# Output stage of the two-slot tiles regrouped: sums of h, state sums, R4 and R5; four sums of the sixth tile on GpSimd

## The chip, the cores and the metric

One NeuronCore of a Trainium2 chip runs the whole kernel in one launch. The metric is device time in microseconds, the median of several runs. Engines are named as in the profile: PE is TensorE (matrix products), DVE is VectorE, ACT is ScalarE, POOL is GpSimd, SP issues the DMAs.

## The reference

A retention recurrence over 4 batches, 8 heads, 768 positions and head size 64, followed by a bilinear feed-forward layer over all 3072 tokens:

```
for t in range(S):
    state = gamma * state + k[:, :, t] outer v[:, :, t]      # per head, 64 x 64
    y[:, :, t] = scale * q[:, :, t] @ state
...
x = y as (3072, 512)
out = ((x @ w_a) * (x @ w_b)) @ w_out                        # d_ff = 1536
```

Inputs and output are float32; the kernel computes products in bfloat16 and adds in float32.

## The kernel before

**Slots and tiles.** The 3072 tokens are 24 slots of 128. `TILES = [4, 2, 2, 2, 2, 4, 4, 4]` groups them into eight tiles, J = 0 to 7; "two-slot tiles" are J = 1 to 4, and the sixth tile is J = 5. J = 2, 3 and 4 follow the same code with a few exceptions for 4. Retention is computed in chunks, two slots at a time, and its result is stored transposed as `xt[J]`, the input of the feed-forward layer of tile J.

**The loop over a tile.** `blocks(J)` goes through twelve steps `ft` (128 columns of d_ff each). In each, `ffn_ab` does `ffn_a` (four products into a PSUM bank "a", cast by ACT to `asb`) and `ffn_g` (four products into a bank "g", which DVE multiplies with `asb` into `ht[J][:, ft]`). Steps in `SPARE` use the attention banks y0 and y1, the others the three rotating banks of the pool `psff`. Then comes the output stage. For tiles in `FAST` it is `ffn_fast(J, u)`, once for each pair of slots u.

**The output stage with seven products.** `ffn_fast` multiplies 2 x 2 blocks with seven products rather than eight (Strassen's scheme in Winograd's form). Each product is six matmuls of 128 x 256. Three use slices of `ht` itself ("h"), four use sums of them ("s", tile `hsum`, four kinds `which` = 0 to 3, each over six column groups f). `add(J, which, f0, f1, eng)` makes the sums for f0 to f1; `adds_of(J, ft)` lists which follow step `ft` (12 is ahead of the output stage, 13 in it, after the first `plus`). The products add into PSUM banks R1, R2, R4 and R5. ACT copies intermediate values of R1 and others to `snap` (`keep`), DVE adds `snap` to a bank into the output tile `osb` (`plus`). R4 exists only for pairs in `ASIDE`; elsewhere its product is the last one, into R1, and ACT copies the result to `osb`. The order with R4 is R1 h00, R2 h10, R4 h11, R1 + s1, R5 s0, R1 + s2, R5 + s3.

**Retention beside it.** `turn(new, old)` does for slots `new` the products of states (`chunk_states`) and scores, and for slots `old` the output products (`inter`, `intra`), which land in the banks y0 and y1. `chunk_states` writes the products to one `psff` bank and to the bank st, and DVE then adds them up into running state sums (`sums`). ACT casts each sum to `gst`, but not at once: the casts wait in a list `later`, and `catch_up(n)` issues the next n of it at given places of the feed-forward code; the two casts of y0 and y1 into `xt` go ahead of them in the list. In the same way the masks of scores wait in `unmasked` for `mask_now`. `casts(t)` scales k and q of slot t and casts v on GpSimd, and issues one transposing DMA on SP; after an odd slot it also issues the loads of the next two.

**What sets the order.** Every instruction goes through `seq`, which chains it to the previous one on its engine: each engine runs in the order in which the program emits. Calls outside the feed-forward loop hang in a table `ahead`, by tile and step, and `visit` runs them there. The tile framework inserts the semaphore waits for data and for buffers that must become free. Tiles 6 and 7 also use seven products for a part of `a` (`SEVEN`, `blocks_seven`), and there some sums of h already run on GpSimd (`sums_of`).

Of the kernel before, what the change touches and what calls it, by code (L numbers as in the profile page):

```python
# [9 lines left out]
F32 = mybir.dt.float32  # L10
BF16 = mybir.dt.bfloat16
AF = mybir.ActivationFunctionType
ALU = mybir.AluOpType
# [1 line left out]

TILES = [4, 2, 2, 2, 2, 4, 4, 4]
FAST = (2, 3, 4, 5, 6, 7)
ASIDE = ((2, 0), (3, 0), (4, 0), (5, 0), (6, 0), (6, 1), (7, 0))
SEVEN = {6: (1, 4), 7: (1, 6)}
SPARE = {(J, ft) for J in (2, 3, 4) for ft in range(1, 6 if J == 4 else 10, 2)}  # L20
PAIRS = 3
# [6 lines left out]
def kernel(  # L28
# [10 lines left out]
    nc = tc.nc  # L39
    P = 128  # L40
    B, H, S, D = q.shape
    NCH = S // P
    HP = H // 2
    DM = H * D
    DFF = moe_w_a.shape[1]
    KT = DM // P
    NFT = DFF // P
# [15 lines left out]
    tra = ctx.enter_context(tc.tile_pool(name="tra", bufs=4))  # L63
# [4 lines left out]
    psat = ctx.enter_context(tc.tile_pool(name="psat", bufs=1, space=bass.MemoryType.PSUM))  # L68
# [6 lines left out]
    def seq(bi):  # L75
        ins = bi.ins
        prev = last.get(ins.engine)
        if prev is not None:
            tc.add_manual_dep(ins, prev.name, nosync, reason="program order")
        last[ins.engine] = ins  # L80
        return bi
# [99 lines left out]
    gst = [const.tile([P, HP, D], BF16, name=f"gst{i}") for i in range(8)]  # L181
# [18 lines left out]
    def cast(engine, dst, src):  # L200
        if engine is nc.scalar:
            seq(nc.scalar.copy(dst, src))  # L202
        else:
            seq(engine.tensor_copy(dst, src))  # L204
# [63 lines left out]
    later = []  # L268
# [6 lines left out]
    sums = {}  # L275

    def chunk_states(n):

        u = [psff.tile([P, 2, HP, D], F32, tag="ff", name="st"),
             psst.tile([P, 2, HP, D], F32, tag="st", name="st")]  # L280
        for s in range(2):
            for hp in range(HP):
                for c in range(2):
                    if (n + s + 1) % NCH == 0 and c == 1:
                        continue
                    for r in range(2):
                        seq(nc.tensor.matmul(u[c][half(r), s, hp, :], kb[n + s][half(c), hp, r, :],  # L287
                                             vb[n + s][half(c), HP * r + hp, :],
                                             start=True, stop=True, skip_group_check=True))
        for s in range(2):  # L290
            t = n + s
            sums[t] = tra.tile([P, 2, HP, D], F32, tag="qk"[s] + "T2", name="sums", bufs=2)
            for c in range(2):
                if (t + 1) % NCH == 0 and c == 1:
                    continue
                new = sums[t][:, c]
                old = sums[t][:, 0] if c else sums.get(t - 1, sums[t])[:, 1]
                if t % NCH == 0 and c == 0:
                    seq(nc.vector.tensor_copy(new, u[c][:, s]))  # L299
                else:  # L300
                    seq(nc.vector.tensor_tensor(new, u[c][:, s], old, op=ALU.add))  # L301
                later.append(lambda i=2 * t + c + 1, new=new: cast(nc.scalar, gst[i % 8], new))

    unmasked = []

# [354 lines left out]
    def add(J, which, f0, f1, eng=nc.vector):  # L660
        if J not in hsum:
            hsum[J] = [wstage.tile([P, NH, 2, P], BF16, tag="w" + "ab"[i % 2], name="hsum") for i in range(4)]
        s = [x[:, f0:f1, : TILES[J] // 2] for x in hsum[J]]
        x, y, op = {
            0: (lambda: rows(J, 0, 1, f0, f1), lambda: rows(J, 1, 1, f0, f1), ALU.add),
            1: (lambda: s[0], lambda: rows(J, 0, 0, f0, f1), ALU.subtract),
            2: (lambda: rows(J, 0, 0, f0, f1), lambda: rows(J, 0, 1, f0, f1), ALU.subtract),
            3: (lambda: rows(J, 1, 0, f0, f1), lambda: s[1], ALU.subtract),
        }[which]
        seq(eng.tensor_tensor(s[which], x(), y(), op=op))  # L670
# [44 lines left out]
    def seven_a(J, f):  # L715

        W2 = 2 * P
        if J not in banks:
            own_banks(J)
        R1, R2, R5 = banks[J][f % 2]  # L720
        snap = raw.tile([P, 4, W2], F32, tag="vf", name="snap")
# [8 lines left out]
        part_a(J, f, R2, 2, True)  # L730
        part_a(J, f, R5, 5, True)
        seq(nc.scalar.copy(snap[:, 2], R5))
        for fn in behind[:1]:
# [41 lines left out]
    def ffn_fast(J, u):  # L775
        osb, dst = placed[J, u] = place(J, u)
        ends = J == len(TILES) - 1 and u == TILES[J] // 2 - 1
        snap = wstage.tile([P, 4, DH], F32, tag="w" + "ba"[u % 2], name="snap")

        def bank():  # L780
            return psff.tile([P, DM], F32, tag="ff", name="o")

        def keep(i, R):
            seq(nc.scalar.copy(snap[:, i], R[:, :DH]))  # L784

        def plus(dst, R, x):
            seq(nc.vector.tensor_tensor(dst, R[:, :DH], x, op=ALU.add))  # L787

        R1, R2 = bank(), bank()
        swap = (J, u) == (7, 0)  # L790
        if swap:
            product(R2, J, u, ("h", 1, 0), (0, 2), True)
        product(R1, J, u, ("h", 0, 0), (0, 0), True)
        keep(0, R1)
        catch_up(2)
        if not swap:
            product(R2, J, u, ("h", 1, 0), (0, 2), True)
        visit(J, "mid")
        plus(osb[:, 0, :DH], R2, snap[:, 0])
        for which, f0, f1 in adds_of(J, NFT + 1):  # L800
            add(J, which, f0, f1)
        mask_now(1)
        catch_up(1)
        store()
        aside = (J, u) in ASIDE
        if aside:
            R4 = bank()
            product(R4, J, u, ("h", 1, 1), (1, 3), True)
            keep(2, R4)
        product(R1, J, u, ("s", 1), (1, 1), False)  # L810
        keep(1, R1)
        catch_up(1)
        visit(J, "sums", u)
        R5 = bank()
        product(R5, J, u, ("s", 0), (1, 0), True)
        keep(3, R5)
        catch_up(1)
        product(R1, J, u, ("s", 2), (1, 2), False)
        if aside:
            seq(nc.vector.tensor_tensor(osb[:, 1].rearrange("p (c d) -> p c d", c=2),  # L820
                                        R1[:, :DH].rearrange("p (c d) -> p c d", c=1).to_broadcast([P, 2, DH]),
                                        snap[:, 2:], op=ALU.add))
        else:
            plus(osb[:, 1, DH:], R1, snap[:, 3])
        if ends:
            seq(nc.sync.dma_start(out=dst[:, 1, DH:], in_=osb[:, 1, DH:]))
        mask_now(1)
        product(R5, J, u, ("s", 3), (0, 3), False)
        plus(osb[:, 0, DH:], R5, snap[:, 1])
        mask_now()  # L830
        if ends:
            seq(nc.sync.dma_start(out=dst[:, 0], in_=osb[:, 0]))
        catch_up(1)
        if not aside:
            product(R1, J, u, ("h", 1, 1), (1, 3), False)
            seq(nc.scalar.copy(osb[:, 1, :DH], R1[:, :DH]))
        if J < len(TILES) - 2:
            held.append((dst, osb))
        elif ends:
            seq(nc.scalar.dma_start(out=dst[:, 1, :DH], in_=osb[:, 1, :DH]))  # L840
        else:
            seq(nc.sync.dma_start(out=dst, in_=osb))

    D_, G_, A_ = nc.vector, nc.gpsimd, nc.scalar
# [100 lines left out]
    for j in range(NO):  # L945
# [8 lines left out]
        (4, 0): [(casts, 17)], (4, 8): [(turn, 14, 12)],  # L954
        (4, "o", 0): [(begin_turn, 14), (casts, 18)], (4, "mid"): [(end_turn, 14), (casts, 19)],
        (5, 0): [(casts, 20)], (5, 2): [(casts, 21)], (5, 3): [(turn, 16, None)],
        (5, 8): [(turn, 18, 16), (casts, 22)],
        (5, "sums", 0): [(turn, 20, 18), (casts, 23)],
        (6, 8): [(turn, 22, 20)], (6, "o", 0): [(turn, None, 22)],
    }  # L960
    ahead[5, "sums", 0] += [(combine_a, f) for f in (1, 2, 3)]
    early = {3: [(0, 0, 2)], 4: [(1, 0, 2)], 5: [(2, 0, 2)], 6: [(3, 0, 2)],
             7: [(0, 2, 4)], 8: [(1, 2, 4)], 9: [(2, 2, 4)], 10: [(3, 2, 4)]}
    adds = {4: {**early, 10: [(3, 2, 4), (0, 4, 5)],
                11: [(1, 4, 5), (0, 5, 6), (1, 5, 6), (2, 4, 5), (2, 5, 6), (3, 4, 5), (3, 5, 6)]},
            2: {**early, 12: [(0, 4, 6), (1, 4, 6)], 13: [(2, 4, 6), (3, 4, 6)]}}

    def visit(*at):
        for fn, *what in ahead.pop(at, ()):
# [2 lines left out]
    def adds_of(J, ft):  # L972
        if J == 4:
            return {4: [(0, 0, 2), (1, 0, 2)], 5: [(2, 0, 2)], 6: [(3, 0, 2)], 10: [(0, 2, 4), (1, 2, 4)],
                    11: [(2, 2, 4), (3, 2, 4)], 12: [(i, 4, 6) for i in range(4)]}.get(ft, ())
        return adds[TILES[J]].get(ft, ())

    def blocks_seven(J):
# [32 lines left out]
    def blocks(J):  # L1011
        done = blocks_seven(J) if J in SEVEN else 0
        for ft in range(done, NFT):
            if ft > 1 or J == 5:
                store()
            visit(J, ft)
            ffn_ab(J, ft)
            if J in FAST:
                for which, f0, f1 in adds_of(J, ft):
                    if J not in SEVEN or f0 >= 4:  # L1020
                        add(J, which, f0, f1)

    combined = {(0, 0): (0, 3), (0, 1): (3, 6)}
    blocks(1)
# [46 lines left out]
```

## Time and profile before

| | |
|---|---|
| median of 3 runs | 221.41 us (221.08 to 221.74) |
| the profiled execution | 221.99 us, of which the span of instructions is 220.3 us |
| PE busy | 212.1 us, 96% of the span |
| DVE busy | 147.8 us, 67% |
| ACT busy | 96.6 us, 44% |
| POOL busy | 116.2 us, 53% |
| granted PE clock | 1.000 |

A row of the timeline has the start in us, the duration, engine, line of the kernel, operation, tiles written and read, form and count (xN: N instructions merged, the duration then goes from the first start to the last end); brackets give the idle time before it and what ended it. A row of a group has the count, the total busy time and the mean duration in ns.

### The profile page before, as it was taken

Reading aid. Unit: us, or ns where it says so; the run is one execution under the profiler, and the core shown is the slowest. Engines: PE = TensorE matmul, PEld = TensorE weight load, DVE = VectorE, ACT = ScalarE, POOL = GpSimd, SP = SyncE. Lnnn points to the kernel's source line nnn. Section 1 sums busy time; section 2 is a strip of 40 time slices with the busy share of each in tenths; the row PEclk is TensorE's granted clock in tenths of the full one; section 3 lists DMA queues with packets and bytes.
Section 4 is the critical chain, followed back from the end, with each engine's and each line's share of the span. In section 5 each row is a group of like instructions: output and inputs, shape, how many; then the busy total and the mean of one; then the engine's idle time right before and its main releaser. Section 6 shows DMA issues by size and latency. Waiting matters only on the chain.

```text
span 220.3 us, 7032 instructions
## 1 busy us (share of the span) xinstructions
PE 212.1 (96%) x2875; PEld 156.5 (71%) x2875; DVE 147.8 (67%) x324; ACT 96.6 (44%) x240; POOL 116.2 (53%) x157
## 2 busy tenths in 40 slices
PE   8889999999999999999999999999999999999993
PEld 7568898886456888887878445478666478666682
DVE  2774456657806687698685489897877694777731
ACT  3665334442426436426466343636432643443231
POOL 6457798682734545054352514536959960087500
PEclk9999999999999999999999999999999999999999
DMA  6999999997999997997868899898800002200022
GB/s 172 346 377 382 369 299 390 342 207 167 216 259 246 233 220 141 128 236 203 191 130 201 230 150 257 156 221 120 237 0 4 0 3 98 97 0 1 3 95 95
DMA packets 94832, 39.77 MB, mean 181 GB/s; under 512 B 76112, under 2 KB 91728, under 8 KB 94800
## 3 DMA queue, kind: packets, MB, share of 16 engines
q1 hardware_dynamic: 94656, 39.20, 70.2%
q8 instruction: 22, 0.36, 0.7%
q10 hardware_dynamic: 144, 0.13, 0.2%
q14 instruction: 10, 0.08, 0.1%
HBM read 28.31 MB, written 6.29 MB: 157 GB/s over the span
## 4 chain that ended last, share of the span: by engine, by line
PE 86%; DVE 5%; DMA 3%; issue 2%; POOL 1%; ACT 1%; SPq 0%; DVEq 0%; POOLq 0%; ACTq 0%
PE g L610 27%; PE a L598 22%; PE o L772 18%; PE o L647 7%; PE a L712 5%; DMA kf<-in_k_dram 3%; DVE ht L613 2%; DVE hsum L670 1%; PE st L287 1%; POOL kqb L239 1%; PE y L359 1%; PE y L371 1%; PE at L317 1%; PE tp L450 1%; PE st L491 1%
## 5 line engine op out<-in xcount | busy, mean ns | idle before, releaser
L613 DVE TENSOR_TENSOR ht<-g,asb 128x256 bf16<-128x256 f32 (+1 forms) x98 | 53.7, 548 | 39.1 <-PE g L610 29.3
L610 PE MATMUL g<-xt,wb_bf 128*128 128x256 bf16 (+1 forms) x432 | 77.7, 308 | 0.3 <-ACT asb L602 0.3
L598 PE MATMUL a<-xt,wa_bf 128*128 128x256 bf16 (+1 forms) x368 | 60.8, 296 | 0.1
L602 ACT CAST asb<-a 128x256 bf16<-128x256 f32 (+1 forms) x82 | 36.8, 450 | 51.4 <-PE a L598 50.8
L610 PEld LDWEIGHTS <-wb_bf 128*128 128x128 bf16 x432 | 42.1, 98 | 16.5 <-issue 0.4
L598 PEld LDWEIGHTS <-wa_bf 128*128 128x128 bf16 x368 | 35.4, 98 | 12.1
L239 POOL TENSOR_TENSOR kqb<-kf,ktab 128x512 bf16<-128x512 f32 x21 | 22.7, 1081 | 40.5 <-DMA kf<-in_k_dram 29.8
L239 POOL TENSOR_TENSOR kqb<-qf,qtab 128x512 bf16<-128x512 f32 x21 | 22.5, 1076 | 6.4 <-DMA qf<-in_q_dram 6.4
L204 POOL CAST vb<-vf 128x512 bf16<-128x512 f32 x24 | 14.8, 624 | 17.8 <-DMA vf<-in_v_dram 13.0
L772 PEld LDWEIGHTS <-hsum 128*128 128x128 bf16 x216 | 21.0, 98 | 4.1 <-DVE hsum L670 0.9
L784 ACT COPY snap<-o 128x256 f32<-128x256 f32 x34 | 12.7, 374 | 21.3 <-PE o L772 19.5
L772 PE MATMUL o<-wt_bf,hsum 128*128 128x256 bf16 x162 | 19.8, 272 | 0.9 <-DVE osb L787 0.5
L670 POOL TENSOR_TENSOR hsum<-ht 128x256 bf16<-128x256 bf16 (+1 forms) x15 | 11.0, 733 | 17.9 <-DVE ht L613 17.9
L772 PEld LDWEIGHTS <-ht 128*128 128x128 bf16 x162 | 15.4, 98 | 2.6
L647 PE MATMUL o<-wo_bf,ht 128*128 128x512 bf16 x72 | 16.1, 379 | 0.0
L670 DVE TENSOR_TENSOR hsum<-ht 128x256 bf16<-128x256 bf16 (+1 forms) x32 | 14.2, 450 | 0.3
L301 DVE TENSOR_TENSOR sums<-st,sums 128x256 f32<-128x256 f32 x30 | 12.7, 423 | 1.5
L772 PE MATMUL o<-wo_bf,ht 128*128 128x256 bf16 x108 | 13.3, 273 | 0.0
L202 ACT CAST gst<-sums 128x256 bf16<-128x256 f32 x33 | 12.6, 412 | 0.5 <-DVE sums L299 0.3
L647 PEld LDWEIGHTS <-ht 128*128 128x128 bf16 x72 | 6.9, 98 | 7.9
L323 DVE TENSOR_TENSOR aT<-at,mask 128x512 bf16<-128x512 f32 x18 | 12.1, 680 | 0.0
L787 DVE TENSOR_TENSOR osb<-o,snap 128x256 f32<-128x256 f32 x20 | 8.3, 416 | 4.8 <-PE o L772 3.2
(99 smaller groups left out, 260.4 us busy)
## 6 DMA issues: line engine op xcount, KB each, us to landing
out_dram<-osb SPq DMA_DIRECT2D x11, 512.0 KB, 3.2
kf<-in_k_dram SPq DMA_DIRECT2D x18, 256.0 KB, 3.9
qf<-in_q_dram SPq DMA_DIRECT2D x36, 128.0 KB, 3.8
vf<-in_v_dram SPq DMA_DIRECT2D x18, 256.0 KB, 4.2
wsta<-in_moe_w_a_dram SPq DMA_DIRECT2D x6, 512.0 KB, 7.6
wstb<-in_moe_w_b_dram SPq DMA_DIRECT2D x6, 512.0 KB, 7.8
wsto<-in_moe_w_out_dram SPq DMA_DIRECT2D x6, 512.0 KB, 8.7
kf<-in_k_dram SPq DMA_DIRECT2D x3, 512.0 KB, 6.1
```

Source lines behind the costliest of these rows:

```text
L202: seq(nc.scalar.copy(dst, src))
L204: seq(engine.tensor_copy(dst, src))
L239: seq(eng.tensor_tensor(dst, src, tab, op=ALU.mult))
L301: seq(nc.vector.tensor_tensor(new, u[c][:, s], old, op=ALU.add))
L598: seq(nc.tensor.matmul(a[:, b0 - c0 : b1 - c0], wa_bf[:, kt, fs], xcols(J, kt, b0, b1), start=(kt == 0 and b0 == c0), stop=(kt == KT - 1 a ...
L602: seq(nc.scalar.copy(asb, a))
L610: seq(nc.tensor.matmul(g[:, b0 - c0 : b1 - c0], wb_bf[:, kt, fs], xcols(J, kt, b0, b1), start=(kt == 0 and b0 == c0), stop=(kt == KT - 1 a ...
L613: seq(nc.vector.tensor_tensor(ht[J][:, ft, c0:c1], g, asbs.pop((J, ft, c0)), op=ALU.mult))
L647: seq(nc.tensor.matmul(o, ht[J][:, ft, i * P : (i + 1) * P], wo_bf[:, f, 2 * r : 2 * r + 2, :].rearrange("p a d -> p (a d)"), start=(ft == ...
L670: seq(eng.tensor_tensor(s[which], x(), y(), op=op))
L772: seq(nc.tensor.matmul(R[:, :DH], lhs, (wo_bf, wt_bf)[w][:, f, m, :], start=(first and f == 0), stop=(f == NH - 1), skip_group_check=True))
L784: seq(nc.scalar.copy(snap[:, i], R[:, :DH]))
```

## The change

- `ASIDE` loses (2, 0) and (3, 0): the output stage of tiles 2 and 3 has no R4, and its product h11 comes last, into R1.
- R5 of tiles 2 and 3 is in the attention bank y0 instead of a `psff` bank.
- The adds that make the state sums of slots 10, 11 and 12, 13 (and with them the entry of their casts in `later`) are put off: they are emitted in the output stage of tiles 2 and 3, after the first `plus`, where sums of h were emitted before (step 13).
- Sums of h of tiles 2 and 3: eight adds of three column groups, after steps 6 to 9 and 12, instead of twelve of two, after steps 3 to 10, 12 and 13.
- Tile 5: the four sums of group f = 4 go to GpSimd at step 10; `casts(22)`, which was at step 8, comes after them at step 11. DVE keeps the four sums of f = 5.
- Tile 6: the sums of kinds 2 and 3 for f = 4 and 5 are made in one add each; six adds on DVE instead of eight.

```diff
-ASIDE = ((2, 0), (3, 0), (4, 0), (5, 0), (6, 0), (6, 1), (7, 0))
+ASIDE = ((4, 0), (5, 0), (6, 0), (6, 1), (7, 0))
...
 def chunk_states(n):
...
-        for s in range(2):
-            t = n + s
-            sums[t] = ...
-            (per chunk: copy or add on DVE, cast appended to later)
+        def sum_up():
+            for s in range(2):
+                (the same)
+        if n in (10, 12):
+            put_off.append(sum_up)
+        else:
+            sum_up()
+    put_off = []
...
 def ffn_fast(J, u):
...
         plus(osb[:, 0, :DH], R2, snap[:, 0])
-        for which, f0, f1 in adds_of(J, NFT + 1):
-            add(J, which, f0, f1)
+        while put_off:
+            put_off.pop()()
         mask_now(1)
         catch_up(1)
...
         visit(J, "sums", u)
-        R5 = bank()
+        R5 = psat.tile([P, DM], F32, tag="y0", name="o") if J in (2, 3) else bank()
...
-        (5, 8): [(turn, 18, 16), (casts, 22)],
+        (5, 8): [(turn, 18, 16)], (5, 10): [(add, 5, i, 4, 5, G_) for i in range(4)], (5, 11): [(casts, 22)],
...
-    adds = {4: {**early, 10: [(3, 2, 4), (0, 4, 5)],
-                11: [(1, 4, 5), (0, 5, 6), (1, 5, 6), (2, 4, 5), (2, 5, 6), (3, 4, 5), (3, 5, 6)]},
-            2: {**early, 12: [(0, 4, 6), (1, 4, 6)], 13: [(2, 4, 6), (3, 4, 6)]}}
+    adds = {4: {**early, 11: [(i, 5, 6) for i in range(4)]},
+            2: {6: [(0, 0, 3)], 7: [(1, 0, 3)], 8: [(2, 0, 3)], 9: [(3, 0, 3)], 12: [(i, 3, 6) for i in range(4)]}}
...
 def adds_of(J, ft):
...
+        if J == 6:
+            return {10: [(0, 4, 5)], 11: [(1, 4, 5), (0, 5, 6), (1, 5, 6), (2, 4, 6), (3, 4, 6)]}.get(ft, ())
...
 def blocks(J):
...
                 for which, f0, f1 in adds_of(J, ft):
-                    if J not in SEVEN or f0 >= 4:
-                        add(J, which, f0, f1)
+                    add(J, which, f0, f1)
```

More of the change, by code (lines that the diff above doesn't have):

```diff
@@ L289, in chunk_states @@
                                              start=True, stop=True, skip_group_check=True))
-        for s in range(2):
-            t = n + s
[L292 to L302, printed above, removed]
+        def sum_up():
+            for s in range(2):
+                t = n + s
+                sums[t] = tra.tile([P, 2, HP, D], F32, tag="qk"[s] + "T2", name="sums", bufs=2)
+                for c in range(2):
+                    if (t + 1) % NCH == 0 and c == 1:
+                        continue
+                    new = sums[t][:, c]
+                    old = sums[t][:, 0] if c else sums.get(t - 1, sums[t])[:, 1]
+                    if t % NCH == 0 and c == 0:
+                        seq(nc.vector.tensor_copy(new, u[c][:, s]))
+                    else:
+                        seq(nc.vector.tensor_tensor(new, u[c][:, s], old, op=ALU.add))
+                    later.append(lambda i=2 * t + c + 1, new=new: cast(nc.scalar, gst[i % 8], new))
+        if n in (10, 12):
+            put_off.append(sum_up)
+        else:
+            sum_up()
+    put_off = []
     unmasked = []
```

## The prediction, made before the changed kernel was run

> **What bounds the kernel now.** I read the page's busy shares first, then the timeline of the output stages that the change touches, with the waits of TensorE (PE) in them.
>
> ```profile
> span 220.3 us, 7032 instructions
> ...
> PE 212.1 (96%) x2875; PEld 156.5 (71%) x2875; DVE 147.8 (67%) x324; ACT 96.6 (44%) x240; POOL 116.2 (53%) x157
> ```
>
> PE is busy for 96% of the span. The change removes no matmul, so it can only take away idle time of PE or add some. I call tiles by the kernel's J: the "sixth tile" is tile 5.
>
> Tile 2, output stage (slots 10 and 11 are turned first); columns are start, duration, engine, line:
>
> ```profile
> 79.84 0.32 PE L359 MATMUL y<-kqT,gst 64*64 64x64 bf16 x16
> 80.01 0.42 DVE L613 TENSOR_TENSOR ht<-g,asb 128x256 bf16<-128x256 f32 x1 [0.25 <-PE g L610]
> 81.17 1.48 PE L772 MATMUL o<-wo_bf,ht 128*128 128x256 bf16 x12
> 82.08 0.37 ACT L784 COPY snap<-o 128x256 f32<-128x256 f32 x1 [1.67 <-DMA kf<-in_k_dram]
> 82.34 1.08 ACT L386 CAST xt<-y 128x512 bf16<-128x512 f32 x2
> 83.30 0.43 ACT L202 CAST gst<-sums 128x256 bf16<-128x256 f32 x1
> 83.60 0.77 ACT L784 COPY snap<-o 128x256 f32<-128x256 f32 x2
> 85.76 0.60 PE L598 MATMUL a<-xt,wa_bf 128*128 128x256 bf16 x4
> ```
>
> From the first output matmul to the next tile are 4.59 us for 42 matmuls: 0.109 each, 0.656 for a product of six. The turn takes 1.33. No wait of PE stands in it: this stage can only get worse.
>
> Tile 3, the same stage (slots 12 and 13):
>
> ```profile
> 93.74 1.04 POOL L239 TENSOR_TENSOR kqb<-kf,ktab 128x512 bf16<-128x512 f32 x1 [5.72 <-DMA kf<-in_k_dram]
> 93.84 1.09 DVE L670 TENSOR_TENSOR hsum<-ht 128x256 bf16<-128x256 bf16 x1
> 95.19 0.79 DVE L670 TENSOR_TENSOR hsum<-hsum,ht 128x256 bf16<-128x256 bf16 x1
> 95.37 0.60 PE L598 MATMUL a<-xt,wa_bf 128*128 128x256 bf16 x4
> 96.99 0.45 PE L287 MATMUL st<-vb,kqb 64*64 64x64 bf16 x32 [0.31 <-DVE ht L613]
> 97.48 0.42 DVE L299 COPY sums<-st 128x256 f32<-128x256 f32 x1
> 98.01 1.34 DVE L301 TENSOR_TENSOR sums<-st,sums 128x256 f32<-128x256 f32 x3
> 98.11 1.48 PE L772 MATMUL o<-wo_bf,ht 128*128 128x256 bf16 x12
> 99.76 1.09 POOL L239 TENSOR_TENSOR kqb<-qf,qtab 128x512 bf16<-128x512 f32 x1
> 99.98 1.01 DVE L670 TENSOR_TENSOR hsum<-hsum,ht 128x256 bf16<-128x256 bf16 x1
> 101.06 1.80 PE L772 MATMUL o<-wt_bf,hsum 128*128 128x256 bf16 x14 [0.37 <-DVE hsum L670]
> 103.35 0.60 PE L598 MATMUL a<-xt,wa_bf 128*128 128x256 bf16 x4
> ```
>
> The last a and g end eight matmuls after 95.37, at 96.24; the turn lasts 1.87 from there instead of 1.33: 0.54 lost, since DVE was late after two slow adds. The products last 5.24, 0.65 too long: the second sum of h came late behind four state sums and GpSimd.
>
> Tile 5, first half of its output stage:
>
> ```profile
> 141.24 0.69 DVE L613 TENSOR_TENSOR ht<-g,asb 128x512 bf16<-128x512 f32 x1
> 144.42 1.47 PE L772 MATMUL o<-wo_bf,ht 128*128 128x256 bf16 x12
> 145.26 1.04 POOL L239 TENSOR_TENSOR kqb<-kf,ktab 128x512 bf16<-128x512 f32 x1 [4.77 <-PE o L772]
> 146.76 1.12 POOL L239 TENSOR_TENSOR kqb<-qf,qtab 128x512 bf16<-128x512 f32 x1 [0.45 <-DMA qf<-in_q_dram]
> 146.90 1.33 DVE L670 TENSOR_TENSOR hsum<-ht 128x256 bf16<-128x256 bf16 x2
> 148.56 0.41 DVE L787 TENSOR_TENSOR osb<-o,snap 128x256 f32<-128x256 f32 x1
> 148.89 1.85 DVE L301 TENSOR_TENSOR sums<-st,sums 128x256 f32<-128x256 f32 x4
> 149.02 1.47 PE L772 MATMUL o<-wt_bf,hsum 128*128 128x256 bf16 x12 [0.49 <-DVE osb L787]
> ```
>
> Four products of six and a turn after 144.42 would be 2.62 and 1.33, that is 148.37; PE goes on at 149.02, 0.65 late. It waits for the bank that the osb addition frees, and that addition stands behind the sums of h.
>
> **The change part by part.** Prices first:
>
> ```profile
> L670 DVE TENSOR_TENSOR hsum<-ht x32: 274/288/1291, 73.5 to 208.9; 128x256 bf16<-128x256 bf16 x27, 128x512 bf16<-128x512 bf16 x5
> 142.45 0.41 DVE L670 TENSOR_TENSOR hsum<-ht 128x512 bf16<-128x512 bf16 x1
> L670 POOL TENSOR_TENSOR hsum<-ht 128x256 bf16<-128x256 bf16 x13 | 8.7, 669 | 15.4 <-DVE ht L613 15.4
> L820 DVE TENSOR_TENSOR osb<-o,snap 128x512 f32<-128x512 f32 x7 | 4.8, 687 | 8.1 <-PE o L772 6.5 <-ACT gst L202 1.6
> L323 DVE TENSOR_TENSOR aT<-at,mask 128x512 bf16<-128x512 f32 x18 | 12.1, 680 | 0.0
> ```
>
> *Eight sums instead of twelve.* Three-wide adds lie between 0.29 (two wide, median) and 0.41 (four wide): 0.35. DVE does 8 x 0.35 = 2.8 for 12 x 0.29 = 3.5. In tile 2 that saves PE nothing: four adds from 80.43 on, one of them perhaps held for a GpSimd multiply (1.0), end by 82.9, and the two that PE wants at 82.48, after two products, by 82.2. In tile 3 the last four also follow the last ht directly, and the wait at 101.06 goes.
>
> *Fifth product's own early bank (R4) gone.* The product h11 moves to the stage's end and adds into R1, after DVE has read R1 there. Tile 5's second half already runs in that form:
>
> ```profile
> 150.99 1.47 PE L772 MATMUL o<-wo_bf,ht 128*128 128x256 bf16 x12
> 154.53 0.42 DVE L787 TENSOR_TENSOR osb<-o,snap 128x256 f32<-128x256 f32 x1 [1.33 <-PE o L772]
> 155.66 1.89 PE L598 MATMUL a<-xt,wa_bf 128*128 128x512 bf16 x8
> ```
>
> It takes 4.67, that is 0.08 over 4.59, which I add in each of the two tiles; it holds what PE waits at the third product for R1's first copy (82.08 to 82.45, wanted at 82.48) as well. On DVE an addition of 0.687 becomes one of 0.41; ACT's copies stay three plus one.
>
> *R5 in bank y0.* The bank is free when ACT's first cast of xt is done, in tile 2 about 82.9; PE wants it two products after 81.17 and one more, 83.14: nothing.
>
> *State sums behind.* This costs. ACT's queue in this stage is: copy of R1 (82.08), two xt casts, a gst cast, then the copy of R1 that lets PE go on adding into R1. The gst cast reads the first state sum, which now comes after the osb addition, and PE no longer has the R4 product to do meanwhile. Tile 2: R2's product ends 1.31 after 81.17; the addition begins 0.25 later (as the copy at 82.08 does behind its product), 82.73; the first sum 0.33 behind that (148.56 to 148.89), 83.06, done 83.48; gst 83.55; the copy 0.30 behind it (83.30 to 83.60), 83.85 to 84.22; PE at 84.30 with 0.07 for each hand-over (DVE's end 100.99 to PE's 101.06). Unhindered it would go on four products after 81.17, at 83.79: 0.51 lost. With the 0.08, tile 2 costs **+0.59**. Ends: +0.08, if the cast does not hold the copy, and +0.8, if the next copy is late too.
>
> Tile 3 has the same 0.51, and four sums of which the first is a copy (97.48 to 99.35, 1.87) from 100.00 to 101.87, then a mask of 0.68 to 102.52, and only then the addition on which h11 waits: PE goes on at 102.97 instead of 102.55, 0.42. So 4.59 + 0.51 + 0.42 = 5.52 against 5.24: **+0.28**. In the turn I take no change: the two adds locked out beside GpSimd (93.84, 95.19) are still there, one wider. Ends: -0.54, if DVE gets through before 93.74, and +0.14, for four adds each 0.07 wider less one that goes; for the products -0.57 (4.67 against 5.24) and +0.28.
>
> *Tile 5.* Four adds go to GpSimd, 4 x 0.669 = 2.7, from the ht that ends at 141.93: done by about 145.0 even with some blocking, before GpSimd's next multiply, which begins at 145.26 with its data (the queue had waited 4.77). So casts(22), moved behind them, lose nothing: two multiplies, a cast and one DMA transpose on SP; they stood waiting in their queues from step 8 on anyway, and SP has no store to do in between. DVE has four adds left after its last ht. The first is shut out by the 145.26 multiply to about 146.45, as now; two more follow 0.3 apart; the fourth meets the 146.76 multiply and ends near 148.0 (the first of the pair at 146.90 does now); the osb addition 147.95 to 148.37; PE at 148.45 instead of 149.02: **-0.57**. Ends: -0.65 (all of the lateness) and +0.1.
>
> The row behind that is the add at 99.98: 1.01 beside a multiply that ends at 100.85. The Trainium skill's "SBUF — State Buffer", section "Who interferes with whom", says that a DVE instruction with two SBUF inputs and a GpSimd instruction reading SBUF exclude each other, the second waiting out the first. The trace agrees, the add ending 0.14 after the multiply. Without the rule, the fourth add ends at 147.2, and the sum would be 0.08 lower.
>
> *Tile 6.* Six adds for eight; PE has no idle time to give there (columns: stretch, its length, PE busy):
>
> ```profile
> 177.35:187.27 9.92, 9.92 (x149) 8.84 (x149) 6.72 (x21) 3.53 (x10) 2.33 (x4) 1.00 0.14 55
> ```
>
> Zero; ends 0 and -0.1 (what precedes it).
>
> **Sum.** +0.59 + 0.28 - 0.57 = +0.30 against the profiled execution's 221.99 (span 220.3, 1.69 around it). The median of the runs is 221.41, 0.58 lower; the same difference on it gives 221.7.
>
> **Rivals.**
> A, faster: the gst cast does not hold the copy in either tile, say because the first sum is done by 83.1. Then tile 2 costs 0.08, tile 3 gains 0.57, tile 5 gains 0.57: -1.06, so 220.35, and with the turn's stall gone too 219.8. For it: two of the three waits do go. Against it: the queue order above.
> B, slower: GpSimd's adds end after 145.3, because DVE's adds shut them out. The multiplies move back with them, and the last adds of h are shut out as late as now; tile 5 gains nothing: +0.87, 222.3. It decides where the four adds take over 3.3 us from 141.93, against 2.7 bare; three DVE adds of 0.4 fall in that time. The skill's rule of the previous part speaks for it, since more GpSimd work means more exclusion.
> C, no measurable change, by another way: tile 3's turn loses its stall, because DVE has three adds fewer before step 6 and passes 93.74 in time. +0.30 - 0.54 = -0.24, 221.2.
>
> **How the numbers follow.** A run here can tell about 0.3%, 0.66 us, from no change: faster is below 220.75, slower above 222.07. Forecast 0.38, C 0.17, A 0.22, B 0.23. So faster 0.22, same 0.55, slower 0.23. The range reaches to A's and B's nearer cases: 220.35 to 222.4, the 0.1 over B for the bound of tile 2.
>
> **What would show it.** Right: in tile 2 and 3 a gst cast directly ahead of ACT's second snap copy, waiting for the sums, and an idle time of PE of about 0.5 after the third and fourth products; in tile 3 one more of 0.4 before h11; in tile 5 no wait of PE for osb over 0.15, and GpSimd's adds ended before its k multiply. Wrong: no idle time of PE behind that copy (A), or tile 5's wait still 0.4 or more (B), or tile 3's turn at 1.4 (C).

## The result and the profile after

The changed kernel takes 222.37 us (median of 11 runs, 221.94 to 223.53) against 221.08 us before in the same comparison: ratio 1.0062, 95% interval 1.0044 to 1.0080. It is about 1.3 us slower, where +0.3 was forecast and no measurable change was given the best chance. The second comparison with the same kernel (e12 below) has 1.0038, 1.0017 to 1.0059.

The page's busy shares of the changed kernel:

```profile
span 220.8 us, 7021 instructions
...
PE 211.8 (96%) x2875; PEld 155.8 (71%) x2875; DVE 144.4 (65%) x310; ACT 96.8 (44%) x240; POOL 118.6 (54%) x161
```

DVE has 3.4 us less to do (147.8 before), PE the same, and the kernel is slower. The waits of PE from 62 to 160 us say where:

```profile
PE o L780 <- ACT snap L792: 1.4, 2, 1.0
PE a L606 <- DVE sums L302: 0.4, 1, 0.4
PE g L618 <- ACT asb L610: 0.3, 1, 0.3
PE st L287 <- DVE osb L795: 0.2, 1, 0.2
```

The waits for hsum and osb that stood before tile 3's and tile 5's products are gone. New ones have come: for ACT's copy (twice, tiles 2 and 3), for state sums in tile 5's steps, and for osb in tile 5 ahead of the turn's state products (st), where it was R5's product that waited before.

The next table is worked out from the timelines: each stage runs from its first PE instruction to the first of the next stage. "Stage" of tiles 2 and 3 is turn plus products; what is not in a column hardly differs.

| kernel | tile 2 stage | tile 3 stage | tile 4 | tile 5 steps | tile 5 output | tile 2's first step to end |
|---|---|---|---|---|---|---|
| before | 5.92 = 1.33 + 4.59 | 6.98 = 1.74 + 5.24 | 18.16 | 22.91 | 11.24 | 151.04 |
| changed | 7.09 = 1.19 + 5.90 | 6.71 = 1.35 + 5.36 | 18.02 | 23.42 | 11.32 | 152.36 |
| changed, second profile (e12) | 6.33 = 1.18 + 5.15 | 7.07 = 1.71 + 5.36 | 18.05 | 22.93 | 11.33 | 151.48 |

The first profile's +1.32 is +1.17 in tile 2, -0.27 in tile 3, -0.14 in tile 4, +0.51 in tile 5's steps, +0.08 in its output stage and -0.03 elsewhere. The spans alone differ by 0.5 only, since the profiled execution of before reached tile 2 0.8 us later.

Timeline of the changed kernel, tile 2's output stage:

```profile
79.98 1.04 POOL L239 TENSOR_TENSOR kqb<-kf,ktab 128x512 bf16<-128x512 f32 x1 [5.34 <-PE y L367]
80.04 1.19 DVE L678 TENSOR_TENSOR hsum<-hsum,ht 128x384 bf16<-128x384 bf16 x1
80.20 1.48 PE L780 MATMUL o<-wo_bf,ht 128*128 128x256 bf16 x12
81.34 1.06 POOL L239 TENSOR_TENSOR kqb<-qf,qtab 128x512 bf16<-128x512 f32 x1 [0.33 <-DMA qf<-in_q_dram]
81.42 1.19 DVE L678 TENSOR_TENSOR hsum<-ht,hsum 128x384 bf16<-128x384 bf16 x1
82.54 0.41 DVE L795 TENSOR_TENSOR osb<-o,snap 128x256 f32<-128x256 f32 x1
82.87 1.33 DVE L302 TENSOR_TENSOR sums<-st,sums 128x256 f32<-128x256 f32 x3
83.32 0.40 ACT L202 CAST gst<-sums 128x256 bf16<-128x256 f32 x1 [0.86 <-DVE sums L302]
83.63 0.37 ACT L792 COPY snap<-o 128x256 f32<-128x256 f32 x1
84.05 0.81 PE L780 MATMUL o<-wt_bf,hsum 128*128 128x256 bf16 x6 [1.05 <-ACT snap L792]
85.45 0.81 PE L780 MATMUL o<-wt_bf,ht 128*128 128x256 bf16 x6
86.10 0.60 PE L606 MATMUL a<-xt,wa_bf 128*128 128x256 bf16 x4
```

The chain is the one forecast: osb addition, first state sum, gst cast that waits 0.86 for it, ACT's copy, PE idle for 1.05. But it starts 0.8 late: two of the four last sums of h took 1.19 instead of 0.35, beside GpSimd's multiplies of 79.98 and 81.34. In the second profile of the same program only one of the four is slow, and early enough to do no harm:

```profile
80.25 1.12 POOL L239 TENSOR_TENSOR kqb<-kf,ktab 128x512 bf16<-128x512 f32 x1 [5.08 <-DMA kf<-in_k_dram]
80.27 1.48 PE L780 MATMUL o<-wo_bf,ht 128*128 128x256 bf16 x12
80.39 1.20 DVE L678 TENSOR_TENSOR hsum<-ht 128x384 bf16<-128x384 bf16 x1
81.51 0.34 DVE L678 TENSOR_TENSOR hsum<-ht,hsum 128x384 bf16<-128x384 bf16 x1
81.60 1.16 POOL L239 TENSOR_TENSOR kqb<-qf,qtab 128x512 bf16<-128x512 f32 x1 [0.23 <-DMA qf<-in_q_dram]
81.85 0.42 DVE L795 TENSOR_TENSOR osb<-o,snap 128x256 f32<-128x256 f32 x1
83.37 0.81 PE L780 MATMUL o<-wt_bf,hsum 128*128 128x256 bf16 x6 [0.29 <-ACT snap L792]
85.42 0.60 PE L606 MATMUL a<-xt,wa_bf 128*128 128x256 bf16 x4
```

That is 5.15 for the products, where the forecast had 5.18: the price of the queue order without GpSimd. The multiply of 81.60 falls on the osb addition here, which takes its usual 0.42.

Timeline of the changed kernel, tile 5, first half of its output stage:

```profile
144.48 0.84 POOL L678 TENSOR_TENSOR hsum<-ht,hsum 128x256 bf16<-128x256 bf16 x1
145.29 1.04 POOL L239 TENSOR_TENSOR kqb<-kf,ktab 128x512 bf16<-128x512 f32 x1
146.29 1.09 POOL L239 TENSOR_TENSOR kqb<-qf,qtab 128x512 bf16<-128x512 f32 x1
146.51 1.02 DVE L678 TENSOR_TENSOR hsum<-hsum,ht 128x256 bf16<-128x256 bf16 x1
147.80 0.31 PE L367 MATMUL y<-kqT,gst 64*64 64x64 bf16 x12
147.85 0.41 DVE L795 TENSOR_TENSOR osb<-o,snap 128x256 f32<-128x256 f32 x1
148.32 0.45 PE L287 MATMUL st<-vb,kqb 64*64 64x64 bf16 x32 [0.21 <-DVE osb L795]
149.48 1.27 PE L780 MATMUL o<-wt_bf,hsum 128*128 128x256 bf16 x10
```

GpSimd's two multiplies follow its adds without a gap, and the second meets DVE's second add, which PE's fourth product needs. PE reaches the turn at 147.80, where 144.82 and four products would be 147.44, and the turn's state products then wait for the bank that the osb addition frees. The second profile has the same wait, though there the second multiply comes later, with its load, and meets only the fourth add:

```profile
146.08 1.04 POOL L239 TENSOR_TENSOR kqb<-qf,qtab 128x512 bf16<-128x512 f32 x1 [0.53 <-DMA qf<-in_q_dram]
146.14 1.13 DVE L678 TENSOR_TENSOR hsum<-ht,hsum 128x256 bf16<-128x256 bf16 x1
147.19 0.41 DVE L795 TENSOR_TENSOR osb<-o,snap 128x256 f32<-128x256 f32 x1
147.66 0.45 PE L287 MATMUL st<-vb,kqb 64*64 64x64 bf16 x32 [0.59 <-DVE osb L795]
148.72 1.49 PE L780 MATMUL o<-wt_bf,hsum 128*128 128x256 bf16 x12
```

In the kernel before, the state products did not wait for that addition; they began 1.2 us ahead of its start at 148.56:

```profile
147.36 0.20 PE L287 MATMUL st<-vb,kqb 64*64 64x64 bf16 x2
```

### The profile page after: what moved, and what is told of

The parts are those of the page before. It is cut to its first block, busy times and chain, and to the rows that moved or that the text cites. A ratio compares the mean times of both kernels' runs of the same rounds, so it can differ in the third digit from the quotient of the medians.

```text
span 220.8 us, 7021 instructions
## 1 busy us (share of the span) xinstructions
PE 211.8 (96%) x2875; PEld 155.8 (71%) x2875; DVE 144.4 (65%) x310; ACT 96.8 (44%) x240; POOL 118.6 (54%) x161
## 4 chain that ended last, share of the span: by engine, by line
PE 85%; DVE 6%; DMA 3%; ACT 2%; POOL 1%; issue 1%; SPq 0%; DVEq 0%; POOLq 0%
PE g L618 27%; PE a L606 22%; PE o L780 16%; PE o L655 7%; PE a L720 5%; DMA kf<-in_k_dram 3%; DVE hsum L678 2%; DVE ht L621 2%; POOL kqb L239 1%; PE y L367 1%; PE at L325 1%; PE y L379 1%; PE st L287 1%; ACT gst L202 1%; DVE osb L795 1%
## 5 line engine op out<-in xcount | busy, mean ns | idle before, releaser
L678 POOL TENSOR_TENSOR hsum<-ht 128x256 bf16<-128x256 bf16 (+1 forms) x17 | 12.3, 725 | 23.0 <-DVE ht L621 23.0
L792 ACT COPY snap<-o 128x256 f32<-128x256 f32 x32 | 11.9, 372 | 20.2 <-PE o L780 20.1
L795 DVE TENSOR_TENSOR osb<-o,snap 128x256 f32<-128x256 f32 x22 | 9.2, 418 | 6.2 <-PE o L780 4.3
L678 DVE TENSOR_TENSOR hsum<-ht 128x256 bf16<-128x256 bf16 (+2 forms) x25 | 11.7, 468 | 0.2
```

## The experiments

Ratios are to the kernel before on the same chip, with their 95% intervals; stage times are of the one profile of each kernel, worked out as in the table.

**e1: the part in tiles 2 and 3 alone.** Against the changed kernel:

```diff
-(5, 8): [(turn, 18, 16)], (5, 10): [(add, 5, i, 4, 5, G_) for i in range(4)], (5, 11): [(casts, 22)],
+(5, 8): [(turn, 18, 16), (casts, 22)],
...
(adds[4] and the list of tile 6 as in the kernel before)
```

> Only the part of the change in tiles 2 and 3; tiles 5 and 6 as before. In the trace of the changed kernel tile 2's output stage is 1.17 us longer than before, tile 3's 0.27 shorter, tile 4 0.14 shorter, the steps of tile 5 0.51 longer and its output 0.08 longer. Theory 1 (each part pays for itself): +0.75 against before, and tile 5's steps as before. Rival (the loss in tile 5's steps is set off by tiles 2 and 3, which shift the loads and GpSimd's multiplies against TensorE): +1.3, with the 0.5 in tile 5's steps still there.

1.0044 (1.0023 to 1.0066), +1.0. Tile 2 6.98, tile 3 7.63, tile 5's steps 23.23, its output 10.70. Most of the loss belongs to tiles 2 and 3. The split of theory 1 isn't right, though: tile 5's steps are 0.32 longer than before with the old code, on the rival's side, and tile 3's stage, the same code as in the changed kernel, is 0.92 longer here. Its timeline:

```profile
97.44 1.15 POOL L239 TENSOR_TENSOR kqb<-kf,ktab 128x512 bf16<-128x512 f32 x1
...
97.73 1.08 DVE L678 TENSOR_TENSOR hsum<-hsum,ht 128x384 bf16<-128x384 bf16 x1
...
98.56 1.15 POOL L239 TENSOR_TENSOR kqb<-qf,qtab 128x512 bf16<-128x512 f32 x1
98.74 1.19 DVE L678 TENSOR_TENSOR hsum<-ht 128x384 bf16<-128x384 bf16 x1
...
99.66 0.73 POOL L204 CAST vb<-vf 128x512 bf16<-128x512 f32 x1
99.86 0.76 DVE L678 TENSOR_TENSOR hsum<-ht,hsum 128x384 bf16<-128x384 bf16 x1
...
102.04 0.81 PE L780 MATMUL o<-wt_bf,hsum 128*128 128x256 bf16 x6 [1.36 <-ACT snap L792]
```

Here GpSimd's cast of v, which stands ahead of these multiplies, began at 96.88 instead of the changed kernel's 98.61, with the turn at the same 96.7; GpSimd worked during the last sums of h rather than behind them, and PE waited 1.36 instead of 0.31.

**e2: the part in tiles 5 and 6 alone.** Against the kernel before:

```diff
-(5, 8): [(turn, 18, 16), (casts, 22)],
+(5, 8): [(turn, 18, 16)], (5, 10): [(add, 5, i, 4, 5, G_) for i in range(4)], (5, 11): [(casts, 22)],
...
(adds[4] and the list of tile 6 as in the change)
```

> Only the part in tiles 5 and 6 (four sums of h on GpSimd, casts(22) behind them, six adds for eight); tiles 2 and 3 as before. My prediction: -0.57. Theory 1 (the part pays for itself): +0.5 to +0.6, with the wait of a for the state sums in step 9 of tile 5 and the sums of h shut out beside GpSimd's multiplies. Rival (set off by tiles 2 and 3): -0.1 to 0 in the output stage and nothing in the steps.

1.0001 (0.9977 to 1.0024): nothing. Output stage of tile 5 11.21, steps 22.95, that is -0.03 and +0.04: the rival's numbers. The forecast gain of 0.57 isn't there.

**e3: ACT's copies ahead of the gst casts** (on e1).

```diff
         mask_now(1)
-        catch_up(1)
+        if J not in (2, 3):
+            catch_up(1)
...
         keep(1, R1)
-        catch_up(1)
+        if J not in (2, 3):
+            catch_up(1)
```

> The part in tiles 2 and 3 again, but ACT's copies of R1 and R5 are ahead of the gst casts in its queue. Theory A (the gst cast that waits for a state sum holds up ACT's copy, and that is the whole cost): 1.0 us better in tile 2 and 0.4 in tile 3, so about -1.3 against the kernel with tiles 2 and 3 alone. Theory D (DVE is late as well: state sums and mask stand ahead of the osb addition that the last product waits for): the wait only moves to the last product; 0.2 better in tile 2, nothing in tile 3.

1.0015 (0.9993 to 1.0038), about 0.6 better than e1, with intervals that overlap. Tile 2 6.71, tile 3 6.85. PE's waits, 62 to 160 us:

```profile
PE o L780 <- DVE osb L795: 1.6, 2, 0.9
```

No wait for ACT is left, and 1.6 us for the osb addition have come in its place: theory D's mechanism. How much of the 0.6 is the order and how much a luckier place of GpSimd's work, this run doesn't tell.

**e4: state sums and first mask behind the osb addition that h11 waits for** (on e3).

```diff
         plus(osb[:, 0, :DH], R2, snap[:, 0])
-        while put_off:
-            put_off.pop()()
-        mask_now(1)
+        if J not in (2, 3):
+            mask_now(1)
...
         keep(3, R5)
-        catch_up(1)
+        if J not in (2, 3):
+            catch_up(1)
...
             plus(osb[:, 1, DH:], R1, snap[:, 3])
+            while put_off:
+                put_off.pop()()
+            if J in (2, 3):
+                catch_up(2)
...
         mask_now(1)
```

> As the kernel with the copies first, and the state sums and the first mask are on DVE only behind the osb addition that the last product waits for. Theory D: tile 2's output stage at most 0.2 longer than before, tile 3's about 0.9 shorter (its turn too), so -1.4 against the kernel with tiles 2 and 3 alone and -0.6 against before. Theory A: the same time as the kernel with the copies first.

1.0040 (1.0021 to 1.0059), where theory D said -0.6 us. The output stages do what it said, 5.88 and 6.07, but tile 3's steps are 11.22 (10.61 before) and tile 4 19.14. From the waits, 62 to 160 us:

```profile
PE a L606 <- DVE osb L795: 1.1, 2, 0.8
```

R5 lies in y0, and step 1 of the next tile wants y0. The osb addition that frees it now stands behind the state sums and a mask. The bank that the prediction gave away free is free only while nothing more is ahead of that addition.

**e5: state sums behind both osb additions** (on e3; casts and masks in the next tile's steps, so the stage's other `mask_now` and `catch_up` are left out for tiles 2 and 3 in the same way).

```diff
-        while put_off:
-            put_off.pop()()
...
         plus(osb[:, 0, DH:], R5, snap[:, 1])
+        while put_off:
+            put_off.pop()()
-        mask_now()
+        if J not in (2, 3):
+            mask_now()
```

> Tiles 2 and 3 with ACT's copies first, and the state sums on DVE behind both osb additions (so that bank y0 is free in time), their casts and the masks in the next tile's steps. If the waits of tiles 2 and 3 are all of the loss: tile 2's output stage (with its turn) 5.9 to 6.0, tile 3's 6.0 to 6.1, nothing in the steps after them, -0.6 to -0.9 against before. Rival (the state sums are work that DVE has no place for: wherever they stand, the next thing behind them is late): the steps of tiles 3 and 4 lose 0.5 to 1.0 as in the kernel with the sums last, and the time is that of before or more.

0.9989 (0.9969 to 1.0009), as before. Tile 2 6.07, tile 3 5.91, as expected, but tile 4 is 18.83 and tile 5's output 11.22. In tile 4's steps two sums of h take 1.01 and 0.79 beside GpSimd's multiplies, and the turn is late for it: the rival's place, by another cause than the rival's. In e2 and e10, whose tiles 2 to 4 have the old code, tile 4 takes 18.76 and 18.69, so this loss can't be put down to the edit.

**e6: GpSimd's scaling held back in tiles 2 and 3** (on e1): the first multiply of slots 12 and 16 gets a dependency on DVE's last sum of h.

```diff
-(2, 7): [(casts, 12)], (2, "o", 0): [(turn, 10, 8), (casts, 13)],
+(2, "o", 0): [(turn, 10, 8)], (2, "mid"): [(hold,), (casts, 12), (casts, 13)],
-(3, "o", 0): [(turn, 12, 10), (casts, 16)],
+(3, "o", 0): [(turn, 12, 10)], (3, "mid"): [(hold,), (casts, 16)],
```

> Tiles 2 and 3 of the change, but GpSimd's scaling of slots 12, 13 and 16 waits for the last sum of h of the tile's output stage, so that it can't shut out those adds. Theory L (the chain from sums of h over the osb addition, the first state sum and the gst cast to ACT's copy hands every exclusion by GpSimd on to TensorE): tile 2's stage 6.3 to 6.5 instead of 7.0, tile 3's 6.6 to 6.7, total +0.1 to +0.4 against before. Theory Q (the order of the queues alone, without GpSimd): as the kernel with tiles 2 and 3 alone, +1.0.

1.0023 (1.0002 to 1.0045), +0.5, half of e1's loss and a little over theory L's range. Tile 2 is 6.33, its products 5.15: the last four sums of h take 0.35 or 0.36 each, as theory L has it. Tile 3 is 7.16: products 5.36 and a turn of 1.80, which waits for sums of h in the steps before. Here the hold is on the wrong slot. The multiplies in tile 3's output stage are slot 15's, which begin at 97.4 to 99.4 in all profiles; slot 16's begin at 104.5 or later in all of them. That slot 15's came behind the last sums of h this time (98.51, the sums done at 98.02) is no work of the hold.

**e7: state sums in the turn again** (on e1).

```diff
-        if n in (10, 12):
+        if False:
             put_off.append(sum_up)
```

> Tiles 2 and 3 of the change, but the state sums are not put off: DVE makes them in the turn, ahead of the last sums of h. Theory P (putting them off is the cost): no wait behind a gst cast; +0.1 to +0.2 against before. Theory R (without the R4 product TensorE has nothing to do while DVE is late, whichever DVE work comes first): it waits for the sums of h instead, 0.4 in tile 2 and 0.9 in tile 3, +0.8 or more against before.

1.0039 (1.0017 to 1.0062): theory R's time, though nearly all of its wait is in tile 3; tile 2's products take 4.94. Tile 3's take 6.30; the timeline has

```profile
101.18 0.50 PE L780 MATMUL o<-wt_bf,hsum 128*128 128x256 bf16 x3 [1.44 <-DVE hsum L678]
```

The first two of the last sums of h take 1.01 and 1.08 there, behind the state sums. So it isn't the putting off alone. Without R4's product PE wants the second sum of h two products after its start instead of three. That this alone costs is argued, not shown: no run takes R4 away by itself, and e8, which keeps it, waits for sums of h too.

**e8: eight sums of h for twelve in the kernel before, nothing else.**

```diff
-            2: {**early, 12: [(0, 4, 6), (1, 4, 6)], 13: [(2, 4, 6), (3, 4, 6)]}}
+            2: {6: [(0, 0, 3)], 7: [(1, 0, 3)], 8: [(2, 0, 3)], 9: [(3, 0, 3)], 12: [(i, 3, 6) for i in range(4)]}}
```

> The kernel before with eight sums of h for twelve in tiles 2 and 3 and nothing else; R4, R5 and the state sums as before. DVE has 0.7 us less to do in each tile, and nothing waits there by the queue order: -0.3 to 0 against before by either theory; +0.3 or more would say that the regrouped sums themselves cost.

1.0061 (1.0032 to 1.0090), a loss as large as that of the whole change and a miss for both theories. Tile 2 6.81, tile 3 7.62, tile 4 18.54, tile 5's steps 23.44. The waits, 62 to 160 us:

```profile
PE o L772 <- DVE osb L787: 1.7, 3, 0.8
PE o L772 <- DVE hsum L670: 0.8, 2, 0.5
```

Twelve sums had left two of the last four behind the osb addition that frees R5's bank (in tile 2, 83.22 and 83.41 against 82.88); now all four are ahead of it, each 0.35 long instead of 0.28 where nothing holds it, and two of them are shut out in tile 2 and three in tile 3. DVE's work went down and PE's wait up. Of the profile's 2.2 us over the kernel before, though, 0.9 lies in tile 4 and tile 5's steps, whose code is the old one, so how much of the loss belongs to the regrouped sums this one profile doesn't say.

**e9: the kernel before with the scaling held** (slots 12, 13, 16 and 22, behind the last sum of h in tiles 2, 3, 5): e6's edit, with `visit(J, "held")` behind the adds of step 13, and

```diff
-(5, 8): [(turn, 18, 16), (casts, 22)],
+(5, 8): [(turn, 18, 16)], (5, "held"): [(hold,), (casts, 22)],
```

> The kernel before, with GpSimd's scaling of slots 12, 13, 16 and 22 held back until the last sum of h of the output stage of tiles 2, 3 and 5. Theory L (time is lost in these stages because GpSimd's multiplies shut out the sums of h): tile 3's stage 6.5 or less instead of 6.98, tile 5's output stage 10.5 to 10.7 in place of 10.6 to 11.2, -0.3 to -0.8 against before. Rival (the scaling then lands on other sums of h and costs the same there): 0 within 0.3.

0.9995 (0.9976 to 1.0014): the rival in time. Tile 5's output is 10.58 as theory L has it, tile 3's stage 7.05, not under 6.5. But theory L wasn't put to the test in tile 3: the multiplies of slot 15, which this run doesn't hold, begin at 98.20 and 99.20 and two of the last sums of h take 0.93 and 1.01 beside them.

**e10: the part in tiles 5 and 6 with casts(22) held** (on e2).

```diff
-(5, 11): [(casts, 22)],
+(5, "held"): [(hold,), (casts, 22)],
```

> The part of the change in tiles 5 and 6, with casts(22) held until tile 5's last sum of h. Theory L (GpSimd's two multiplies come back to back behind its four adds and shut out the last sums of h of DVE): tile 5's output stage 10.5 to 10.6 instead of 11.2, so -0.6 against the part without the hold. Rival (the bank that the turn's state products take is late by itself): 11.0 or more.

0.9971 (0.9956 to 0.9987). Tile 5's output 10.58, 0.63 less than in e2: theory L. Its timeline, where the four adds now take 0.29 each and the multiply comes behind them:

```profile
144.40 0.29 DVE L677 TENSOR_TENSOR hsum<-ht 128x256 bf16<-128x256 bf16 x1
144.72 0.29 DVE L677 TENSOR_TENSOR hsum<-hsum,ht 128x256 bf16<-128x256 bf16 x1
144.93 0.28 DVE L677 TENSOR_TENSOR hsum<-ht 128x256 bf16<-128x256 bf16 x1
145.13 0.28 DVE L677 TENSOR_TENSOR hsum<-ht,hsum 128x256 bf16<-128x256 bf16 x1
145.83 1.04 POOL L244 TENSOR_TENSOR kqb<-kf,ktab 128x512 bf16<-128x512 f32 x1 [1.93 <-DVE osb L794]
```

**e11: e5 with the scaling held in tiles 2, 3 and 5**, by the edits of e9, with the visit ahead of the osb addition.

> The kernel with the state sums behind both osb additions, with GpSimd's scaling held back in tiles 2, 3 and 5 as well. Theory L: tiles 2 and 3 as without the hold (6.1 and 5.9), tile 5's output stage 10.5 to 10.7, -0.8 to -0.3 against before. Rival (what is gained in a stage is lost in the next where GpSimd's work meets DVE): within 0.3 of before.

0.9953 (0.9935 to 0.9970), 220.33 against 221.03: faster than both kernels, -0.7 as theory L has it. Tile 2 6.02, tile 3 6.17, tile 4 18.18, tile 5's output 10.59. The hold on slot 16 changes nothing here either; slot 15's multiplies (98.19) happened to begin behind tile 3's last sum of h. One wait of PE of 0.2 or more is left between 62 and 160 us, and it was there before:

```profile
PE g L625 <- ACT asb L617: 0.3, 1, 0.3
```

**e12: the changed kernel again**, not edited.

> The changed kernel once more, for a second profile of it. If the stages are set by where GpSimd's multiplies happen to fall: tile 3's stage anywhere from 6.7 to 7.6 and tile 5's steps from 22.9 to 23.4, tile 2's 6.9 to 7.1, tile 5's output 11.2 to 11.3. If the first profile's stages are fixed costs: each within 0.1 of it. The time +1.0 to +1.4 against before in either case.

1.0038 (1.0017 to 1.0059), +0.8, less than was expected. Tile 2's stage 6.33, under the forecast band, tile 3's 7.07, tile 5's steps 22.93: up to 0.8 from the first profile, in both directions. The stages are not fixed costs. Tile 5's output repeats, at 11.33, though GpSimd's second multiply fell on another add.

## Why the prediction was right and wrong

*Right: state sums behind.* The gst cast held ACT's copy for the first state sum, as worked out. Where GpSimd does no harm the products take 5.15 in tile 2 (e6, e12) against 5.18 forecast. In tile 3 they take 5.36 in three profiles (the two of the change and e6) against 5.52: state sums and mask took 2.39 instead of 2.52, and h11 came 0.29 late instead of 0.42. The sum for tile 3 leaves out the 0.08 that the text says it adds in each tile; with it, 5.60 and +0.38 in all. Tile 6 gave nothing, as forecast: from its first step to the end are 64.6 us in both kernels.

*Mis-sized: tile 2, by its last sums of h.* I let them end by 82.9 with one of them held, saw that the two that PE wants are in time, and put their cost at nothing. But they stand ahead of the osb addition, the head of the very chain that I priced next, and I started that chain at R2's end instead. Two of four held cost 0.75 more in the first profile (5.90); one held early cost nothing in the second. e6 shows that GpSimd is the cause: with it held 5.15, against 5.67 in e1, the same kernel without the hold. The term for the products is +0.56 or +1.31 in the two profiles, where I had +0.59, depending on where GpSimd's multiplies fall.

*Wrong: tile 5's -0.57.* The step that failed is "PE at 148.45": it had R5, behind the turn, wait for the bank that the osb addition frees, as before. In the three profiles with the change's code of tile 5 (its two and e2) it is the turn's state products that wait for it, and 1.05 to 1.16 us of the turn stand behind them. The addition itself ended earlier than forecast, 3.44 to 3.56 after the first output product instead of 3.95, and still R5 began 4.55 to 4.68 after it instead of 4.03. Had only R5 waited, it would have begun with the turn's end, at 3.93 to 4.19; this is an estimate from the turn's start in each profile and the 1.21 that the turn takes without a wait (e10). So the place of the wait cost 0.37 to 0.75, and I had it at nothing. That it comes with the change is seen in the profiles: with the old code the state products begin before the addition has ended, as shown above for the kernel before, and in e1 (148.38 against 148.93). Which part of the change moved it, the order of the sums or that of casts(22), no run separates.

"Lose nothing" failed as well for casts(22). I took 145.26 and 146.76, the arrival of two loads in one execution, for fixed times. Where data come sooner, GpSimd's adds hold the first multiply and release it onto the last sums of h; the second follows at once in two of the three profiles. The output stage takes 11.32, 11.33 and 11.21. With the multiplies held (e10) the addition ends at 2.36, ahead of the state products at 2.82, nothing waits for it, and the stage takes 10.58. The stage that I compared with was no fixed cost either: the eight profiles with the old code of tile 5 and casts(22) not held have 10.58 to 11.24, mean 10.87, and mine was the longest. Against that mean the part costs 0.4.

*Not priced: tile 5's steps.* Of the first profile's +1.32, 0.51 lie there. A sum of h takes 1.31 at 136.94, beside the multiply of 136.93, and the turn's state sums come behind it, for which PE then waits 0.41. In the second profile that sum takes 0.43 and the steps 22.93; e8 has the loss with tile 5's old code.

*Neither: tile 3's turn.* I took no change and gave the other case to rival C. It was 1.35 in one profile and 1.71 in the other: C in one of the two. The old code varies there as well, 1.74 before and 1.28 in e2 and e10. Rival B named GpSimd's exclusion in tile 5 and nearly the right time (222.3), but put the decision on adds that take over 3.3; they took 3.0 in both profiles and tile 5 gained nothing all the same. Its time is in part luck: it has no term for tile 5's steps. The exclusion itself held: the add of 81.42 ends at 82.61, 0.21 after the multiply's 82.40, as in the row of before. The Trainium skill's "SBUF — State Buffer", section "Who interferes with whom", says that a DVE instruction with two SBUF inputs and a GpSimd instruction that reads SBUF contend; the trace agrees.

*Left open.* The medians say +1.3 and +0.8 for the same program in two comparisons. Each run's loads arrive differently, and one profile a kernel doesn't show how often each case comes. R4's loss and R5's move to y0 were never run by themselves.

## What to carry to other kernels

A stall beside work that is paced by DMA is a draw: before a gain is booked on it, find the same code's stall in a second profile. When an engine's work is reordered, price the whole queue ahead of each instruction that another engine waits for, also where the work in it shrinks (e8). Ask as well which instruction will come to wait for a buffer that another engine frees: the earlier it stands in its queue, the sooner the buffer has to be free (tile 5). Work that can shut out a critical instruction can be tied behind it with a dependency (tile 2 in e6, tile 5 in e10), but see first in the trace which piece of work does the harm: in tile 3 it was slot 15's, and slot 16's was tied.

## What the runs showed of the hardware that I had not expected

Adds in a row on DVE can each be shut out by one of several GpSimd instructions in a row: GpSimd starts its next one before DVE's next add (e1: multiplies at 97.44 and 98.56 and a cast at 99.66; adds at 97.73, 98.74 and 99.86). The three adds took 1.08, 1.19 and 0.76 instead of 0.35 each. The osb addition, which reads one operand from a PSUM bank, took its usual 0.42 beside a multiply (e12, 81.85 beside 81.60).
